# Denominators of linear attention: one row per head, spread over partitions by a DMA through DRAM

## The chip, the cores and the metric

The kernel runs on one core of one Trainium2 chip. The metric is the device time of one execution in microseconds (us). A run is an execution; where several were made, the median is quoted with the lowest and highest. A ratio is the mean time of one kernel's fast runs over the mean time of the other kernel's fast runs of the same rounds, so it is not quite the ratio of the medians that are quoted. A run counts as slow when it lies over 1.5% above the fastest run of the same kernel.

Engine names in the profile lines: PE is TensorE, PEld its weight loads, DVE VectorE, ACT ScalarE, POOL GpSimd, SP SyncE, which here only issues DMAs. A q after the name (SPq, ACTq) marks the issuing of DMAs.

## The reference

The block is adaLN, linear attention, adaLN, and a GEGLU feed-forward layer; S = 2048 tokens, D = 1024, 32 heads of 32, F = 3584. What matters here is the middle:

```python
pq, pk = (phi(q), phi(k))                       # per head: s x d, all positive
kv  = jnp.einsum('bhsd,bhse->bhde', pk, v)
z   = jnp.einsum('bhsd->bhd', pk)
num = jnp.einsum('bhqd,bhde->bhqe', pq, kv)
den = jnp.einsum('bhqd,bhd->bhq', pq, z)[..., None] + 1e-06
o   = num / den                                 # one denominator per token and head
x   = x + ga * (o.transpose(...).reshape(B, S, D) @ wo)
```

The kernel multiplies the transposed query features by 1/den, merges kv with wo into one 1024 x 1024 matrix ("the merge"), and runs one projection for all heads. There are 2048 x 32 denominators, but the product needs each of them on the 32 partitions of its head.

## The kernel before

Every operation is first recorded in a plan. A list scheduler with a cost model then orders the operations of VectorE, ScalarE, GpSimd and SyncE in 16 rounds and keeps the order that its model likes best; TensorE's order is as recorded. The program issues each engine's operations in exactly that order. Below it is called the recorded order.

```python
KEEP = 0.7                                     # damping of the due times from round to round
...
for i in range(2 * self.ROUNDS):
    forward(i >= self.ROUNDS)                  # keeps the best order of all rounds
...
return [self.ops[n] for _, n in best[1]]
```

The denominators, two groups of 128 query features by 512 tokens at a time:

```python
def den_pair(b, g, banks):                     # called 16 times
    psd = banks.pair()
    for i in range(2):                         # Dbd: block diagonal, z of each head repeated in 32 columns
        te.matmul(psd[:, i, :], lhsT=Dbd[:, g + i, :], rhs=pqT[b][:, g + i, :], start=True, stop=True)
    ac.activation(out=psd, in_=psd, func=AF.Ln, bias=eps6, scale=1.0)
    rden = rden_ring()
    ac.activation(out=rden, in_=psd, func=AF.Exp, scale=-1.0)      # 1/den = exp(-ln(den))
    o = pqT[b][:, g:g + 2, :]
    tt_op(o, o, rden, ALU.mult)
```

The matmul does the spreading: its result has each denominator on all 32 partitions of the head. Five of the 16 pairs stand in the merge, eleven in the projection:

```python
for i, stage in enumerate(stages):             # the merge, beside the last query products
    ...
    if 6 <= i < 6 + KD:
        if i in (6, 8, 10, 12, 13):
            den_pair(*den_todo.pop(0), psN)
        wp_step(i - 6)
...
for tt in range(NTT):                          # the projection, 16 tiles of 128 tokens
    if den_todo:
        den_pair(*den_todo.pop(0), psX)
    xt = wo_tile(tt, psX if tt == 0 else psC)  # loads x on SP, 16 matmuls, x + result on VectorE, store of x2
```

A projection tile takes its buffer from `x2_ring`, whose slots begin at 191 KB of each partition; the first tiles of the next stage (the row sums of the down weights, "b11") begin at 174 KB.

Of the kernel before, what the change touches and what calls it, by code (L numbers as in the profile page):

```python
# [11 lines left out]
BF16 = mybir.dt.bfloat16  # L12
F16 = mybir.dt.float16
AF = mybir.ActivationFunctionType
ALU = mybir.AluOpType
# [262 lines left out]
def kernel(  # L278
# [14 lines left out]
    P = 128  # L293
# [4 lines left out]
    S, D = x_in.shape  # L298
    F = B_w_gate.shape[1]
    KD = D // P  # L300
    JF = F // P
    TG = 512
    NG = S // TG
# [8 lines left out]
    DH = D // H  # L312
# [5 lines left out]
    KH = KD // 2  # L318
    NPR = JF // 2
    MW = 4 * NW  # L320
# [55 lines left out]
    def at(off, shape, dt):  # L376
        return Ring(off, shape, dt, 1)()
# [3 lines left out]
    maskbd = at(0.25, [P], F16)  # L381
# [20 lines left out]
    eps6 = at(1.78125, [1], FP32)  # L402
# [11 lines left out]
    srep = at(2.75, [KD, DH], BF16)  # L414
    garow = at(3.5, [D], F16)
    gbrow = at(3.5, [D], F16)
    Dbd = at(7.5, [KD, P], F16)
    mrow_ring = Ring(9.5, [NW], F16, 2)
    c8 = at(11.5, [P], BF16)

# [15 lines left out]
    pqT = [pq2[b // 2][:, b % 2] for b in range(4)]  # L436
# [7 lines left out]
    for o in (3.5, 194.25, 7.5, 120):  # L444
        wm1_ring.slots += Ring(o, [MW], BF16, 1).slots
    wm2_ring = Ring(27.75, [MW], BF16, 4)
    wm2_ring.slots += Ring(152, [MW], BF16, 3).slots + Ring(53, [MW], BF16, 1).slots
    qf_ring = Ring(176, [2, TG], FP32, 3)
    Wo_sb = at(11.75, [KD, D], BF16)
    ph_ring = Ring(198.25, [2, TG], F16, 4)  # L450
# [1 line left out]
    kvzacc = at(190, [KD, P + 1], FP32)  # L452
    KVbd = at(194.25, [KD, P], F16)
    KVbdT = at(196.25, [KD, P], F16)
    rden_ring = Ring(44, [2, TG], BF16, 3)
    bst_ring = Ring(206.25, [NBN, nc.vector.BN_STATS_DIM], FP32, 4)
    mv_ring = Ring(206.5, [nc.vector.BN_AGGR_DIM], FP32, 8)
    rstd_ring = Ring(206.625, [1], FP32, 8)
# [5 lines left out]
    def quarters(n, shape, dt):  # L464
# [25 lines left out]
    sub_a = [at(76 + 3.5 * j, [NPR // 2, HB], F16) for j in range(3)]  # L490
    sub_b = [at(189 + 3.5 * j, [NPR // 2, HB], F16) for j in range(4)]
    x2_ring = Ring(191, [D], BF16, 4)
    x2e_ring = Ring(144, [D], BF16, 3)
    xhe_ring = Ring(150, [D], F16, 3)
    junk = at(156, [D], BF16)
# [9 lines left out]
    psX, psW, psN = Banks(4, 7), Banks(4, 5), Banks(6, 7)  # L505
    psC, psB = Banks(0, 3), Banks(4, 7)

    scr_pool = ctx.enter_context(tc.tile_pool(name="scr", bufs=1, space=bass.MemoryType.DRAM))
    xh_scr = [[scr_pool.tile([TG, D], F16, name=f"xhs{g}_{h}", tag=f"xhs{g}_{h}") for h in range(2)]
              for g in range(NGR)]  # L510
    xa_scr = [scr_pool.tile([TG, D], F16, name=f"xas{b}", tag=f"xas{b}") for b in range(NG)]
    x2_scr = [scr_pool.tile([TG, D], BF16, name=f"x2s{b}", tag=f"x2s{b}") for b in range(NG)]
    t_scr = scr_pool.tile([P, 4, NPR, NW], F16, name="ts", tag="ts")
    u_scr = scr_pool.tile([P, NPR // 2, 3, 4, HB], F16, name="us", tag="us")
# [7 lines left out]
    te, ve, ac, gp, sy = (plan.on(e) for e in ("PE", "DVE", "ACT", "POOL", "SP"))  # L522
# [12 lines left out]
    def tt_op(out, a, b, op):  # L535
        ve.tensor_tensor(out=out, in0=a, in1=b, op=op)  # L536
# [410 lines left out]
    def kv_products(b, kb):  # L947
        glo, ghi = kb * GPB, min(KD, (kb + 1) * GPB)
        kvps = (psKV1 if b == 0 else psKV if b == 3 else QB)()[:, 0:GPB * (P + 1)].rearrange("p (g e) -> p g e", e=P + 1)
        for tl in range(TT):  # L950
            for g in range(glo, ghi):
                te.matmul(kvps[:, g - glo, :], lhsT=pks[b, tl // 2][:, tl % 2, g * P:(g + 1) * P],  # L952
                                 rhs=vta[:, tl][:, g, 0:P + 1], start=(tl == 0 and g == glo), stop=(tl == TT - 1),
                                 skip_group_check=True)
        src = kvps[:, 0:ghi - glo, :]
        if b == 0:
            ve.tensor_copy(out=kvzacc[:, glo:ghi, :], in_=src)
        else:
            tt_op(kvzacc[:, glo:ghi, :], src, kvzacc[:, glo:ghi, :], ALU.add)

    def den_pair(b, g, banks):
        psd = banks.pair()
        for i in range(2):
            te.matmul(psd[:, i, :], lhsT=Dbd[:, g + i, :], rhs=pqT[b][:, g + i, :], start=True, stop=True)
        ac.activation(out=psd, in_=psd, func=AF.Ln, bias=eps6, scale=1.0)  # L965
        rden = rden_ring()
        ac.activation(out=rden, in_=psd, func=AF.Exp, scale=-1.0)  # L967
        o = pqT[b][:, g:g + 2, :]
        tt_op(o, o, rden, ALU.mult)

    den_todo = [(b, g) for b in range(NG) for g in range(0, KD, 2)]

    def wp_step(g):
        psw = psW.pair()
        for h in range(2):
            te.matmul(psw[:, h, :], lhsT=KVbdT[:, g, :], rhs=Wo_sb[:, g, h * NW:(h + 1) * NW], start=True, stop=True)
        ve.scalar_tensor_tensor(out=Wp[:, g, :], in0=psw.rearrange("p h n -> p (h n)"), scalar=1.0 / GA_SCALE,
                                in1=garow, op0=ALU.mult, op1=ALU.mult)

    def kv_diagonal():  # L980
        for g in range(KD):
            ve.tensor_scalar_mul(out=Dbd[:, g, :], in0=maskbd, scalar1=kvzacc[:, g, P:P + 1])
        tt_op(KVbd, kvzacc[:, :, 0:P], maskbd[:, None, :].to_broadcast((P, KD, P)), ALU.mult)

    def kv_transposes():
        for half in range(2):
            psk = psX(F16)[:, 0:NW].rearrange("p (g e) -> p g e", e=P)
            for g in range(4):
                te.transpose(psk[:, g, :], KVbd[:, half * 4 + g, :], ident)
            ve.tensor_copy(out=KVbdT[:, half * 4:half * 4 + 4, :], in_=psk)  # L990
# [18 lines left out]
    def wd_moves(seen_of, n):  # L1009


        if not wd_todo:
            return
        plan.hold([op for op in plan.ops if op.eng == "PE"][-1])
        gp.tensor_copy(out=seen, in_=seen_of)
        plan.hold(plan.ops[-1])
        for dst, src, add in wd_todo[:n]:
            move(dst, src, add)
        del wd_todo[:n]
        plan.hold()  # L1020
# [98 lines left out]
    def ln2_xhat(tt, x2, mv, rstd):  # L1119
        g, h, tl = tt // (2 * TT), tt // TT % 2, tt % TT  # L1120
        xh = xh2_ring()
        ve.tensor_scalar(out=xh, in0=x2, scalar1=mv[:, 0:1], scalar2=rstd[:, 0:1],
                                op0=ALU.subtract, op1=ALU.mult)
        gp.dma_start(out=xh_scr[g][h][tl * P:(tl + 1) * P, :], in_=xh)
        if tl == TT - 1:
            h2_load(g, h)
# [44 lines left out]
    def wo_tile(tt, banks):  # L1171
        b, tl = tt // TT, tt % TT
        xt = x2_ring()
        sy.dma_start(out=xt, in_=x_in[tt * P:(tt + 1) * P, :])
        psw = banks.pair()
        for half in range(NHD):
            for g in range(KD):
                te.matmul(psw[:, half, :], lhsT=pqT[b][:, g, tl * P:(tl + 1) * P],  # L1178
                          rhs=Wp[:, g, half * NW:(half + 1) * NW], start=(g == 0), stop=(g == KD - 1))
        tt_op(xt, psw.rearrange("p h n -> p (h n)"), xt, ALU.add)  # L1180
        gp.dma_start(out=x2_scr[b][tl * P:(tl + 1) * P, :], in_=xt)
        return xt

    def merge_phase(stages):

        ms1 = ModSet(1, wm1_ring, psK)
        sy.dma_start(out=Wo_sb, in_=A_wo.rearrange("(kd p) n -> p kd n", p=P))
        for i, stage in enumerate(stages):
            if i < NKB:
                kv_products(NG - 1, i)  # L1190
            if i in (0, 2):
                for _ in range(KH):
                    ms1.step()
            if i == 3:
                ms2 = ModSet(2, wm2_ring, psN)
                ms1.columns()
            if i == 4:
                ms1.spread(0, garow, GA_SCALE)
                kv_diagonal()
            if i == 5:  # L1200
                kv_transposes()
            if i == 12:
                ms2.columns()
                ve.tensor_scalar_add(out=opcB, in0=modT[:, 4 * KD:5 * KD], scalar1=1.0)
            if 6 <= i < 6 + KD:
                if i in (6, 8, 10, 12, 13):
                    den_pair(*den_todo.pop(0), psN)
                wp_step(i - 6)
            if i == 11:
                for _ in range(KD):  # L1210
                    ms2.step()
            stage(())
            if 7 <= i < 11:
                wd_moves(Wp[:, i - 7, 0:1], 3)
        return lambda: ms2.spread(2, gbrow, 1.0)
# [3 lines left out]
    def wo_phase(gate_rows):  # L1219
        plan.transpose = (6000, 1000000)  # L1220
        fill = [None] * NTT
        fill[9] = h2_mods[0][0]
        fill[11] = h2_mods[0][1]
        fill[12] = h2_steps
        for tt in range(NTT):
            if den_todo:
                den_pair(*den_todo.pop(0), psX)
            xt = wo_tile(tt, psX if tt == 0 else psC)
            for h in range(2):
                if tt == AIM[h]:  # L1230
                    plan.aim(h2_loads[0, h])
            if tt == NTT - 2:
                gate_rows()
            if tt < 2 * TT:
                ln2_xhat(tt, xt, *ln2_stats(xt, act_rstd))
            for f in fill[tt] or []:
                f()
# [483 lines left out]
```

## Time and profile before

757.8 us, median of 3 runs (757.32 to 763.23).

| what | value | view |
|---|---|---|
| TensorE busy | 734.4 of 754.9 us (97%) | busy table |
| granted clock | 1.0 in every stretch | table of windows |
| TensorE idle from 165 to 254 us (merge end and projection) | 4.0 us | table of windows |
| 32 denominator matmuls | 0.216 us each when back to back, 6.9 us | timeline |
| 16 Ln and 16 Exp of 128x1024 | 1088 and 1024 ns, 33.8 us | source lines |

The head of the profile page, with the busy time and the forty slices in tenths:

```profile
span 754.9 us, 11379 instructions
...
PE 734.4 (97%) x4144; PEld 391.3 (52%) x4164; DVE 623.4 (83%) x1304; ACT 411.6 (55%) x697; POOL 95.8 (13%) x175
...
PE   5999999998999999999999999999999999999997
...
PEclk9999999999999999999999999999999999999999
```

The table of windows of the same run. Columns: the stretch in us, its length, busy us of each engine with instructions in brackets, granted clock, DMA share, GB/s:

```profile
165.00:195.00 30.00, 26.79 (x152) 12.01 (x153) 26.28 (x39) 25.59 (x28) 15.08 (x16) 1.00 0.78 130
195.00:254.00 59.00, 58.19 (x268) 26.41 (x270) 49.08 (x81) 36.27 (x53) 11.98 (x22) 1.00 0.86 253
254.00:754.00 500.00, 495.02 (x2854) 279.10 (x2856) 415.56 (x887) 250.96 (x485) 29.12 (x50) 1.00 0.58 180
```

254 us is where the first gate matmul of the feed-forward layer begins (253.7 by the timeline). I call what lies ahead of it "early" and what follows "late"; they sum to the span, up to rounding. The early part ends here after 253.7 us and the late one takes 501.3 us. In these two windows TensorE has 4.0 us of gaps in 89, so nearly all of its work counts in full; ScalarE has room.

The groups of waits by TensorE (engine and line, what it waited for: us in total, times, longest):

```profile
PE psum L964 <- ACT mem L967: 1.9, 2, 1.0
...
PE psum L1178 <- DVE mem L536: 0.7, 1, 0.7
```

L964 is the denominator matmul, L967 the Exp, L1178 the projection matmul, L536 a helper that records VectorE's products and sums. That is nearly all that TensorE waits in this part.

### The profile page before, as it was taken

To read this page: it belongs to the slowest core of one execution; us is meant where nothing else is said; L and a number is where in the kernel's file an instruction comes from. 1 tells how busy PE (TensorE), PEld (TensorE's weight loads), DVE (VectorE), ACT (ScalarE), POOL (GpSimd) and SP (SyncE) were. 2 spreads that over 40 slices of the span, in tenths; PEclk is the share of its full clock that TensorE was granted. 3 is DMA by queue.
4 is the path that set the end of the run, shared out by engine and by line. 5 is a ranking of instruction groups with operands and counts; after the bars stand their busy time and mean duration, and the time that the engine had idled before them with its cause. 6 is when DMAs were issued, how large, how long until landed. Compare 5 with 4: busy or idle time off the path is not lost.

```text
span 754.9 us, 11379 instructions
## 1 busy us (share of the span) xinstructions
PE 734.4 (97%) x4144; PEld 391.3 (52%) x4164; DVE 623.4 (83%) x1304; ACT 411.6 (55%) x697; POOL 95.8 (13%) x175
## 2 busy tenths in 40 slices
PE   5999999998999999999999999999999999999997
PEld 2454544453444444444545486645555555548664
DVE  7898986579897788988998689678888899998763
ACT  3675675668866578766755243016666667621000
POOL 2331332007121003101100001010000000000000
PEclk9999999999999999999999999999999999999999
DMA  9848166789389647687652999752322313399822
GB/s 314 305 120 252 43 151 155 277 309 167 86 231 315 232 154 246 220 272 281 207 185 60 292 276 313 254 181 84 112 78 90 112 56 112 103 274 294 280 95 80
DMA packets 140760, 144.78 MB, mean 192 GB/s; under 512 B 33441, under 2 KB 120865, under 8 KB 139937
## 3 DMA queue, kind: packets, MB, share of 16 engines
q1 hardware_dynamic: 124016, 106.31, 46.8%
q0 software_dynamic: 14336, 35.66, 14.9%
q10 hardware_dynamic: 2352, 2.10, 0.8%
q8 instruction: 32, 0.52, 0.3%
q14 instruction: 24, 0.19, 0.1%
HBM read 111.81 MB, written 32.24 MB: 191 GB/s over the span
## 4 chain that ended last, share of the span: by engine, by line
PE 80%; DVE 8%; ACT 6%; DMA 4%; issue 1%; SPq 1%; DVEq 0%; ACTq 0%
PE psum L1286 28%; PE psum L1489 13%; PE psum L1533 9%; PE psum L1297 7%; DVE mem L536 7%; PE psum L838 6%; PE psum L1178 6%; PE psum L908 4%; PE psum L937 4%; DMA mem<-in_A_wqkv_dram 2%; DMA mem<-in_B_w_up_dram 1%; DMA mem<-in_w_mod_dram 1%; PE psum L952 1%; ACT psum L965 1%; ACT mem L967 1%
## 5 line engine op out<-in xcount | busy, mean ns | idle before, releaser
L536 DVE TENSOR_TENSOR mem<-mem 128x512 f16<-128x512 f16 (+11 forms) x633 | 292.5, 506 | 12.1 <-ACT mem L967 2.5
L1286 PE MATMUL psum<-mem 128*128 128x512 f16 x1248 | 299.3, 379 | 1.3 <-ACT psum L1340 0.5
L536 DVE TENSOR_TENSOR mem<-psum,mem 128x512 f16<-128x512 f32 (+4 forms) x260 | 192.3, 748 | 67.5 <-ACT mem L783 22.6
L783 ACT ACTIVATE mem<-psum 128x256 f32<-128x256 f32 (+2 forms) x228 | 123.2, 555 | 121.1 <-PE psum L1533 46.4
L1286 PEld LDWEIGHTS <-mem 128*128 128x128 f16 (+1 forms) x1248 | 122.0, 98 | 113.4 <-issue 4.0
L1489 PE MATMUL psum<-mem 128*128 128x512 f16 (+2 forms) x458 | 99.0, 372 | 0.7 <-DVE mem L536 0.5
L1297 PE MATMUL psum<-mem 128*128 128x256 f16 x560 | 89.5, 272 | 0.3
L1297 PEld LDWEIGHTS <-mem 128*128 128x128 f16 (+1 forms) x560 | 54.7, 98 | 45.7 <-issue 3.9
L1489 PEld LDWEIGHTS <-mem 128*128 128x128 f16 x462 | 45.1, 98 | 49.9 <-issue 0.7
L1533 PE MATMUL psum<-mem 128*128 128x256 f16 (+1 forms) x588 | 66.2, 273 | 0.0
L1340 ACT ACTIVATE psum<-psum 128x512 f32<-128x512 f32 x56 | 33.0, 589 | 59.0 <-PE psum L1286 31.5
L1533 PEld LDWEIGHTS <-mem 128*128 128x128 f16 x588 | 57.5, 98 | 9.2
L838 PE MATMUL psum<-mem 128*128 128x512 f16 (+1 forms) x272 | 61.6, 379 | 0.4
L1178 PE MATMUL psum<-mem 128*128 128x512 f16 x256 | 57.4, 379 | 0.8 <-DVE mem L536 0.7
L908 PE MATMUL psum<-mem 128*128 128x512 f16 x224 | 51.1, 379 | 0.1
L536 DVE TENSOR_TENSOR psum<-psum,mem 128x256 f32<-128x256 f32 x80 | 34.2, 427 | 12.3 <-ACT mem L783 12.2
L1357 ACT ACTIVATE mem<-psum 128x512 f16<-128x512 f32 x56 | 33.2, 598 | 18.8 <-PE psum L1286 18.3
L838 PEld LDWEIGHTS <-mem 128*128 128x128 f16 x280 | 27.1, 98 | 31.2
L1178 PEld LDWEIGHTS <-mem 128*128 128x128 bf16 x256 | 25.0, 98 | 31.0 <-issue 0.9
L1367 ACT ACTIVATE mem<-mem 128x512 f16<-128x512 f16 x56 | 34.9, 633 | 2.0 <-DVE mem L536 1.8
L908 PEld LDWEIGHTS <-mem 128*128 128x128 f16 (+1 forms) x224 | 21.5, 98 | 26.8 <-issue 2.1
L614 DVE BATCH_NORM_STATS2 mem<-mem 128x6 f32<-128x512 bf16 x48 | 31.0, 678 | 1.6 <-DMA mem<-in_A_x_dram 1.6
(126 smaller groups left out, 558.5 us busy)
## 6 DMA issues: line engine op xcount, KB each, us to landing
mem<-in_B_w_gate_dram SPq DMA_DIRECT2D x14, 1024.0 KB, 6.1
mem<-in_B_w_up_dram SPq DMA_DIRECT2D x14, 1024.0 KB, 5.8
mem<-in_w_mod_dram SPq DMA_DIRECT2D x24, 512.0 KB, 7.0
mem<-us SPq DMA_DIRECT2D x24, 448.0 KB, 8.0
mem<-in_A_x_dram SPq DMA_DIRECT2D x32, 256.0 KB, 4.0
ts<-in_B_w_down_dram POOLq DMA_DIRECT2D x28, 256.0 KB, 6.7
us<-mem POOLq DMA_DIRECT2D x7, 768.0 KB, 7.2
mem<-in_B_w_down_dram SPq DMA_DIRECT2D x12, 448.0 KB, 6.8
```

The lines of the kernel that those rows point to most:

```text
L536: ve.tensor_tensor(out=out, in0=a, in1=b, op=op)
L783: ac.activation(out=t, in_=ps, func=AF.Copy)
L838: te.matmul(ps, lhsT=A[:, k, i * P:(i + 1) * P], rhs=B[:, k, :], start=(start and k == 0), stop=(k == KH - 1), skip_group_check=True)
L908: te.matmul(o, lhsT=W[:, k, (j0 + i) * P:(j0 + i + 1) * P], rhs=h_form(a, k), start=(start and k == 0), stop=(k == KH - 1), skip_group_che ...
L1178: te.matmul(psw[:, half, :], lhsT=pqT[b][:, g, tl * P:(tl + 1) * P], rhs=Wp[:, g, half * NW:(half + 1) * NW], start=(g == 0), stop=(g == K ...
L1286: te.matmul(ps, lhsT=a[:, k, e, :], rhs=b[:, k, :], start=(start and k == 0), stop=(k == KH - 1), skip_group_check=True)
L1297: te.matmul(ps, lhsT=self.x[a][:, k, :], rhs=self.y[y][:, k, :], start=(start and k == 0), stop=(k == KH // 2 - 1), skip_group_check=True)
L1340: ac.activation(out=z, in_=x, func=AF.Copy)
L1357: ac.activation(out=o, in_=ps, func=AF.Gelu_apprx_tanh)
L1367: ac.activation(out=o, in_=o, func=AF.Gelu_apprx_tanh)
L1489: te.matmul(psm[:, q, c], lhsT=A[:, i, q * P:(q + 1) * P], rhs=wt[:, i, c], start=(start and i == 0), stop=(i == NPR - 1), skip_group_chec ...
L1533: te.matmul(ps[:, q, :], lhsT=a[:, k, q * P:(q + 1) * P], rhs=y[:, k, :], start=(start and q == 0 and k == 0), stop=(k == NPR // 2 - 1), s ...
```

## The change

The intent: compute each denominator once, in one row per head, take Ln and Exp there, and let the DMA engines do the spreading. The new weights `zc` have 32 columns, so four sums fill the 128 partitions of one result, and 2 blocks of 512 tokens go through one pair of activations of 128x512. The inverses are stored to DRAM as [4 rows x 2048] for each block and half of the features. A load reads each row 32 times, 512 KB in all, into 128 partitions.

```diff
-    Dbd = at(7.5, [KD, P], F16)
+    zc = at(7.5, [KD, DH], F16)
+    rdc = at(8.5, [TG], BF16)
...
-    rden_ring = Ring(44, [2, TG], BF16, 3)
+    rden_ring = Ring(44, [KH, TG], BF16, 2)
+    rden_ring.slots += Ring(56, [KH, TG], BF16, 1).slots
...
     x2_ring = Ring(191, [D], BF16, 4)
+    x2_ring.slots += Ring(176, [D], BF16, 4).slots
...
+    def den_sums(pr, ps):                        # pr: the pair of token blocks
+        for gi in range(KH):
+            for b in range(2):
+                for half in range(2):
+                    o, g = DH * (2 * b + half), KH * half + gi
+                    te.matmul(ps[o:o + DH, :], lhsT=zc[:, g, :], rhs=pqT[2 * pr + b][:, g, :],
+                              start=(gi == 0), stop=(gi == KH - 1))
+        ac.activation(out=ps, in_=ps, func=AF.Ln, bias=eps6, scale=1.0)
+        ac.activation(out=rdc, in_=ps, func=AF.Exp, scale=-1.0)
+        for b in range(2):
+            for half in range(2):
+                o = DH * (2 * b + half)
+                sy.dma_start(out=den_scr[pr][b, half].rearrange("j (g t) -> (j g) t", g=KH),
+                             in_=rdc[o:o + KH * P // DH, :])
+
+    def den_mul(b, half):
         rden = rden_ring()
+        src = den_scr[b // 2][b % 2, half]
+        sy.dma_start(out=rden.rearrange("p g t -> p (g t)"),
+                     in_=src[:, None, :].to_broadcast((P // DH, DH, KH * TG)))
+        for i in range(0, KH, 2):
+            o = pqT[b][:, KH * half + i:KH * half + i + 2, :]
+            tt_op(o, o, rden[:, i:i + 2, :], ALU.mult)
...
-                if i in (6, 8, 10, 12, 13):
-                    den_pair(*den_todo.pop(0), psN)
+                if i == 6:
+                    den_sums(0, psN())
+                if i in (9, 11, 13):
+                    den_mul(*den_todo.pop(0))
...
-            if den_todo:
-                den_pair(*den_todo.pop(0), psX)
+            if tt == 1:
+                den_sums(1, psX())
+            if tt in (0, 2, 3, 5, 6):
+                den_mul(*den_todo.pop(0))
```

Cut: the DRAM scratch, the fill of `zc`, one moved slot of a weight ring, and the removed lines of `den_pair`, which is printed above.

More of the change, by code (lines that the diff above doesn't have):

```diff
@@ L446 @@
     wm2_ring = Ring(27.75, [MW], BF16, 4)
-    wm2_ring.slots += Ring(152, [MW], BF16, 3).slots + Ring(53, [MW], BF16, 1).slots
+    wm2_ring.slots += Ring(152, [MW], BF16, 3).slots + Ring(52, [MW], BF16, 1).slots
     qf_ring = Ring(176, [2, TG], FP32, 3)
@@ L511 @@
     xa_scr = [scr_pool.tile([TG, D], F16, name=f"xas{b}", tag=f"xas{b}") for b in range(NG)]
+    den_scr = [scr_pool.tile([2, 2, P // DH, KH * TG], BF16, name=f"den{pr}", tag=f"den{pr}") for pr in range(2)]
     x2_scr = [scr_pool.tile([TG, D], BF16, name=f"x2s{b}", tag=f"x2s{b}") for b in range(NG)]
@@ L959, in kv_products @@
             tt_op(kvzacc[:, glo:ghi, :], src, kvzacc[:, glo:ghi, :], ALU.add)
-    def den_pair(b, g, banks):
-        psd = banks.pair()
-        for i in range(2):
-            te.matmul(psd[:, i, :], lhsT=Dbd[:, g + i, :], rhs=pqT[b][:, g + i, :], start=True, stop=True)
-        ac.activation(out=psd, in_=psd, func=AF.Ln, bias=eps6, scale=1.0)
-        rden = rden_ring()
-        ac.activation(out=rden, in_=psd, func=AF.Exp, scale=-1.0)
-        o = pqT[b][:, g:g + 2, :]
-        tt_op(o, o, rden, ALU.mult)
-    den_todo = [(b, g) for b in range(NG) for g in range(0, KD, 2)]
+    def den_sums(pr, ps):
[13 more added lines that the diff above has]
+    def den_mul(b, half):
+        rden = rden_ring()
+        src = den_scr[b // 2][b % 2, half]
[4 more added lines that the diff above has]
+            tt_op(o, o, rden[:, i:i + 2, :], ALU.mult)
+    den_todo = [(b, half) for b in range(NG) for half in range(2)]
     def wp_step(g):
@@ L980, in kv_diagonal @@
     def kv_diagonal():
+        gp.memset(zc, 0.0)
         for g in range(KD):
-            ve.tensor_scalar_mul(out=Dbd[:, g, :], in0=maskbd, scalar1=kvzacc[:, g, P:P + 1])
+            ve.tensor_scalar_mul(out=zc[:, g, g % KH:KH * P // DH:KH], in0=maskbd[:, 0:P:DH], scalar1=kvzacc[:, g, P:P + 1])
         tt_op(KVbd, kvzacc[:, :, 0:P], maskbd[:, None, :].to_broadcast((P, KD, P)), ALU.mult)
```

## The prediction

> **What bounds the kernel now.** TensorE: in the page's busy table PE has 734.4 us of a 754.9 us span (97%). By the table of windows PE is idle 8.8 us in the first 20 us, 3.2 in the last 14, and 3.2 from 165 to 195 us, where the merge of the output weights runs beside the last query products. From 195 to 255 us, in the output projection, it is idle 0.8 us. The denominators live in these last two stretches; there VectorE is busy 26.3 of 30 us and 50 of 60, ScalarE 25.6 and 36.
>
> **What the change removes.**
> - ScalarE: 16 pairs of Ln (1088 ns) and Exp (1024 ns), 33.8 us. Four activations of 128x512 come instead, about 0.6 us each here: 2.4 us.
> - TensorE: 32 matmuls of 128x512 at 0.216 us (the timeline shows 0.43 us per pair between projection groups), 6.9 us. Instead, 32 matmuls with 32 output columns[...]. The modulation's 32 matmuls of 128*32 took 1.91 us. [...] TensorE saves 5.0 us: 1.2 in the merge, 3.8 in the projection.
> - VectorE: the 16 products of 128x1024 (0.68 us) stay; the diagonal's eight small products shrink, under 1 us.
>
> **What it adds.** Eight small stores and eight loads of 512 KB that spread the rows, all on SP's queue. Loads of 256 to 512 KB took 3.7 to 7.4 us from issue to landing in this window. From sum to first product: about 1.2 us of activations, 2 to 4 of store, 4 to 7 of load, 8 to 11 in all. The sums are issued at the sixth step, near 167 us; the first product stands on VectorE before the sixth of eight merge steps, near 177. That is tight, and the weight moves keep the DMA share at 0.7 to 1.2 then.
>
> **How much is critical.** In the projection PE has no gaps, so its 3.8 us count in full if VectorE follows: of a 3.88 us period it idles about 0.3, and at 3.45 it becomes the tighter engine for the first eight tiles. It can catch up in the last eight, which have no normalisation; but the second half's transposed rows come 1 to 2 us later against PE, with some 3 us of slack before the gate products. In the merge, 1.2 us of PE work and the waits on the Exp (1.9 + 0.2) go; VectorE's floor of about 27 us keeps part. The 0.7 us wait on VectorE near 239 us may go. The 31 us of ScalarE are mostly worth nothing.
>
> Sum: -5.0 (PE work), -2.5 (waits), +1.5 (new waits) = -6 us.
>
> **Prediction: 751.5 us, 747.5 to 756.** Faster by over 2%: 0.02; within 2%: 0.97; slower: 0.01.
>
> **What would show it.** Den matmuls under 2.5 us in all; ScalarE 31 us lower; PE 5 us lower; no PE wait on the Exp; projection tiles 3.45 us apart; VectorE waiting under 3 us on the spread rows; gate products from about 247 instead of 253.7 us, the rest unchanged within 1 us.
>
> **What would make it wrong.** The first spread load landing late, so that VectorE and the merge stop for several us; stores and loads holding up SP's queue before input tiles or transposes; the new recorded order costing time in the gate and up stage.

The 5.0 us of TensorE are 6.9 us less the 1.91 us that before's trace shows for 32 matmuls of 128*32. The 2 to 4 us of store were a guess of mine; no trace is named for them.

## The result, and the profile after

787.88 us median (787.28 to 790.06, 4 runs) against 758.66 before: ratio 1.0379, 95% interval 1.033 to 1.0428. The change made the kernel 3.8% slower. The result is correct.

The head of the page after:

```profile
span 788.3 us, 11367 instructions
...
PE 742.3 (94%) x4148; PEld 391.1 (50%) x4164; DVE 623.2 (79%) x1304; ACT 381.9 (48%) x669; POOL 96.5 (12%) x176
...
PE   5999999996977799999999999999999999999997
...
PEclk9999999998988899999999999999999999999999
```

ScalarE lost 29.7 us, as foreseen. But TensorE's busy time rose by 7.9 us although it has less to do, and slices 10 to 14 have gaps or a lower clock. The table of windows after, cut at the same events (the first gate matmul begins at 280.7 us):

```profile
165.00:195.00 30.00, 22.65 (x131) 9.07 (x131) 18.60 (x27) 12.55 (x15) 14.95 (x16) 0.89 0.81 154
195.00:281.00 86.00, 68.85 (x286) 28.70 (x286) 50.67 (x82) 19.34 (x37) 12.30 (x22) 0.88 0.79 207
281.00:788.00 507.00, 495.71 (x2854) 278.93 (x2856) 420.76 (x898) 251.01 (x486) 30.51 (x50) 1.00 0.57 179
```

The early part is 27.0 us longer. TensorE is busy 22.65 + 68.85 = 91.5 us there instead of 26.79 + 58.19 = 85.0, so 6.5 us of the 27 are busy time and 20.5 idle time. The late part is 6.3 us longer at the same busy time.

The waits of TensorE and VectorE after:

```profile
PE psum L1198 <- DVE mem L540: 15.9, 4, 7.2
...
PE psum L568 <- DVE mem L563: 4.8, 1, 4.8
PE psum L995 <- DVE mem L996: 3.2, 3, 2.5
```

```profile
DVE mem L540 <- DMA mem<-den: 31.8, 6, 7.4
```

L1198 is now the projection, L995 the merge, L568 a small matmul of the modulation, L540 the helper. The wait of 31.8 us by VectorE is for the spread rows. It didn't exist before, and I had allowed it 3 us. The timeline of VectorE shows the first two of the six:

```profile
179.68 0.41 DVE L782 TENSOR_SCALAR mem<-mem 128x1024 f16<-128x1024 f16 x1
185.21 0.69 DVE L540 TENSOR_TENSOR mem<-mem 128x1024 bf16<-128x1024 bf16 x1 [5.12 <-DMA mem<-den]
...
193.47 0.69 DVE L540 TENSOR_TENSOR mem<-mem 128x1024 bf16<-128x1024 bf16 x1 [4.63 <-DMA mem<-den]
```

And the queue that issues, SP, at the same time (L978 the stores, L984 the spread loads, L1194 the x tiles):

```profile
170.89 1.74 SPq L978 DMA_DIRECT2D den<-mem  x4
172.74 3.37 SPq L984 DMA_DIRECT2D mem<-den  x2
...
206.40 1.72 SPq L978 DMA_DIRECT2D den<-mem  x4
...
218.88 1.16 SPq L984 DMA_DIRECT2D mem<-den  x2
```

The first load was issued at 172.74 and its product began at 185.21, 12.5 us later; the load was what the product waited for. For the second pair of blocks the stores alone landed 12.1 to 12.5 us after they were issued, and the loads could be issued only then; why the stores were so slow wasn't taken apart.

TensorE's timeline shows the second effect. After a stall, 16 projection matmuls took 6.56 us; before, 16 of them took 3.62 us (from the start of the first to the end of the last). The table of windows gives 0.50 as the granted clock around the end of the first stall (184.1 to 188.9 us):

```profile
231.71 6.56 PE L1198 MATMUL psum<-mem 128*128 128x512 f16 x16 [5.84 <-DVE mem L540]
240.97 12.21 PE L1198 MATMUL psum<-mem 128*128 128x512 f16 x48 [2.69 <-DVE mem L540]
260.40 9.33 PE L1198 MATMUL psum<-mem 128*128 128x512 f16 x32 [7.23 <-DVE mem L540]
```

```profile
186.60:193.30 6.70, 4.17 (x13) 1.60 (x15) 2.23 (x4) 0.00 (x0) 0.73 (x1) 0.50 1.03 213
```

In the clock records of the trace there are five stretches at 0.5, of 6.83, 3.41, 6.83, 3.41 and 6.83 us, 27.3 us in all. Each begins in the last 2.4 us of one of TensorE's five stalls of over 2 us, or at most 0.8 us after it. They account for the busy time: 6.5 us more, although 4.8 us of matmul work are gone (below), makes 11.3 us; and TensorE is busy for 21.7 us of these 27.3, of which half, 10.8 us, is what half clock adds.

### The profile page after: what moved, and what is told of

Same layout as the page of the kernel before. It is cut to its first block, busy times and chain, and to the rows that moved or that the text cites. A ratio compares the mean times of both kernels' runs of the same rounds, so it can differ in the third digit from the quotient of the medians.

```text
span 788.3 us, 11367 instructions
## 1 busy us (share of the span) xinstructions
PE 742.3 (94%) x4148; PEld 391.1 (50%) x4164; DVE 623.2 (79%) x1304; ACT 381.9 (48%) x669; POOL 96.5 (12%) x176
## 4 chain that ended last, share of the span: by engine, by line
PE 49%; DMA 8%; DVE 6%; ACT 4%; issue 1%; SPq 0%; DVEq 0%; ACTq 0%
PE psum L1310 24%; PE psum L1513 12%; PE psum L1557 6%; PE psum L1321 6%; DVE mem L540 5%; DMA mem<-xhs 4%; DMA mem<-x2s 2%; DMA mem<-in_B_w_up_dram 1%; PE psum L1198 1%; ACT mem L787 1%; ACT mem L1178 1%; DVE psum L540 1%; ACT psum L1364 1%; ACT mem L1163 1%; ACT mem L1159 0%
## 5 line engine op out<-in xcount | busy, mean ns | idle before, releaser
L540 DVE TENSOR_TENSOR mem<-mem 128x1024 f16<-128x1024 bf16 (+11 forms) x633 | 294.6, 507 | 46.9 <-DMA mem<-den 31.8
L1310 PE MATMUL psum<-mem 128*128 128x512 f16 x1248 | 299.6, 379 | 3.2 <-ACT mem L787 1.6
L540 DVE TENSOR_TENSOR mem<-psum,mem 128x512 f16<-128x512 f32 (+4 forms) x260 | 192.3, 748 | 62.1 <-ACT mem L787 24.4
L787 ACT ACTIVATE mem<-psum 128x256 f32<-128x256 f32 (+2 forms) x228 | 123.3, 554 | 119.2 <-PE psum L1557 46.8
L1198 PE MATMUL psum<-mem 128*128 128x512 f16 x256 | 63.7, 413 | 15.9 <-DVE mem L540 15.9
L1557 PEld LDWEIGHTS <-mem 128*128 128x128 f16 x588 | 57.5, 98 | 11.3 <-issue 2.1
L912 PE MATMUL psum<-mem 128*128 128x512 f16 x224 | 54.2, 395 | 0.2
L1198 PEld LDWEIGHTS <-mem 128*128 128x128 bf16 x256 | 26.7, 105 | 52.8 <-issue 27.8
L540 DVE TENSOR_TENSOR psum<-psum,mem 128x256 f32<-128x256 f32 x80 | 34.2, 427 | 14.7 <-ACT mem L787 14.4
## 6 DMA issues: line engine op xcount, KB each, us to landing
mem<-in_A_x_dram SPq DMA_DIRECT2D x32, 256.0 KB, 9.4
ts<-in_B_w_down_dram POOLq DMA_DIRECT2D x28, 256.0 KB, 7.0
```

Source lines behind the costliest of these rows:

```text
L540: ve.tensor_tensor(out=out, in0=a, in1=b, op=op)
L787: ac.activation(out=t, in_=ps, func=AF.Copy)
L912: te.matmul(o, lhsT=W[:, k, (j0 + i) * P:(j0 + i + 1) * P], rhs=h_form(a, k), start=(start and k == 0), stop=(k == KH - 1), skip_group_che ...
L1198: te.matmul(psw[:, half, :], lhsT=pqT[b][:, g, tl * P:(tl + 1) * P], rhs=Wp[:, g, half * NW:(half + 1) * NW], start=(g == 0), stop=(g == K ...
L1310: te.matmul(ps, lhsT=a[:, k, e, :], rhs=b[:, k, :], start=(start and k == 0), stop=(k == KH - 1), skip_group_check=True)
L1557: te.matmul(ps[:, q, :], lhsT=a[:, k, q * P:(q + 1) * P], rhs=y[:, k, :], start=(start and q == 0 and k == 0), stop=(k == NPR // 2 - 1), s ...
```

## The experiments

The first theory, A in the expectations: the load's shape makes it slow. Its source has 4 rows, and between 180 and 192 us its packets (4096 bytes each, about 172 ns) are never more than 4 at a time. Theory A supposes that more source rows bring more packets in flight and a faster load; the change's trace alone doesn't show that. (The trace doesn't name a packet's engine, so how many DMA engines carry the load isn't shown.) The rivals: the repeated reading of the same rows of DRAM; the queue of SP; and the recorded order, which the scheduler made anew for the whole kernel.

A table of all runs comes first; "early" and "late" are read from the profiled run of each, and the medians of before in its five batches of rounds are 758.94 (e1 to e4), 757.02 (e5 to e8), 758.13 (e9 to e11), 757.97 (e12 to e14) and 757.77 (e15, e16). The batches ran on four different chips, so times of different batches are best compared by their ratios to before.

| run | median us (lowest to highest) | ratio to before [95%] | early | late |
|---|---|---|---|---|
| before | 758.66 (757.32 to 763.23) | 1 | 253.7 | 501.3 |
| the change | 787.88 (787.28 to 790.06) | 1.0379 [1.033, 1.0428] | 280.7 | 507.6 |
| e1 no spread | 768.60 (767.76 to 775.16) | 1.0139 [1.0088, 1.019] | 249.7 | 516.8 |
| e2 8 rows | 777.33 (776.09 to 780.43) | 1.0241 [1.0204, 1.0278] | 266.9 | 507.4 |
| e3 16 rows | 767.26 (763.22 to 772.81) | 1.0118 [1.0051, 1.0184] | 252.6 | 511.0 |
| e4 4 loads of one row | 771.20 (769.68 to 773.53) | 1.0157 [1.0121, 1.0194] | 264.4 | 507.4 |
| e5 no spread, old late order | 761.63 (759.27 to 762.34) | 1.0054 [1.0029, 1.0078] | 257.5 | 501.7 |
| e6 16 rows, old late order | 766.09 (764.37 to 767.77) | 1.0118 [1.0092, 1.0143] | 259.7 | 503.0 |
| e7 the change, old late order | 792.29 (789.7 to 796.53) | 1.0469 [1.0431, 1.0507] | 287.5 | 507.3 |
| e8 before, other order | 774.45 (763.83 to 782.93) | 1.0144 [1.0077, 1.0211] | 252.8 | 517.7 |
| e9 no spread, whole old order | 758.85 (757.75 to 762.12) | 1.0021 [0.9983, 1.0058] | 256.0 | 500.6 |
| e10 16 rows, whole old order | 771.48 (769.38 to 776.86) | 1.0187 [1.0141, 1.0234] | 267.9 | 500.6 |
| e11 the change, whole old order | 796.35 (794.02 to 796.84) | 1.0498 [1.0471, 1.0526] | 290.3 | 504.8 |
| e12 no spread, four slots | 754.91 (753.74 to 758.67) | 0.9955 [0.9899, 1.001] | 249.2 | 502.6 |
| e13 16 rows, ACT's queue | 773.51 (771.41 to 774.89) | 1.0189 [1.0135, 1.0243] | 266.2 | 503.4 |
| e14 16 rows, SP and ACT | 762.79 (762.32 to 764.86) | 1.0059 [0.9998, 1.012] | 259.7 | 500.8 |
| e15 16 rows, SP and POOL | 757.68 (755.32 to 763.08) | 1.0002 [0.9959, 1.0046] | 260.1 | 501.2 |
| e16 e15, gate products moved | 755.87 (754.21 to 761.06) | 0.9961 [0.9939, 0.9983] | 255.1 | 504.2 |

### The load itself: e1, e2, e3, e4

e1 takes the stores and loads away. The product multiplies the tile by itself instead, with the same instruction, so its result is wrong.

```diff
-                sy.dma_start(out=den_scr[pr][b, half].rearrange("j (g t) -> (j g) t", g=KH),
-                             in_=rdc[o:o + KH * P // DH, :])
...
-        sy.dma_start(out=rden.rearrange("p g t -> p (g t)"),
-                     in_=src[:, None, :].to_broadcast((P // DH, DH, KH * TG)))
...
-            tt_op(o, o, rden[:, i:i + 2, :], ALU.mult)
+            tt_op(o, o, o, ALU.mult)
```

> No stores, no spread loads; each product multiplies a tile with itself (wrong result on purpose, same size and count of VectorE work). All theories in which the spread's DMA is the cause expect the compute part alone to be a gain: 749 to 753 us, PE busy about 729 us, no stall over 1 us between 165 and 240 us, clock 1.0. A rival in which the compact sums themselves, the 32-column matmuls or the new recorded order cost the time expects over 775 us.

e2 and e3 keep the 512 KB load and give its source 8 and 16 rows, by storing each head's row two or four times; the sum makes two copies by two equal columns of `zc`, and e3 stores twice.

```diff
-    den_scr = [scr_pool.tile([2, 2, P // DH, KH * TG], ...
+    den_scr = [scr_pool.tile([2, 2, 4 * P // DH, KH * TG], ...      # e2: 2 * P // DH
...
-                sy.dma_start(out=den_scr[pr][b, half].rearrange("j (g t) -> (j g) t", g=KH),
-                             in_=rdc[o:o + KH * P // DH, :])
+                for s in range(2):
+                    sy.dma_start(out=den_scr[pr][b, half].rearrange("(j s r) (g t) -> s j (r g) t", s=2, r=2, g=KH)[s],
+                                 in_=rdc[o:o + DH, :])
...
-                     in_=src[:, None, :].to_broadcast((P // DH, DH, KH * TG)))
+                     in_=src[:, None, :].to_broadcast((4 * P // DH, DH // 4, KH * TG)))
```

> Each compact row is stored twice, so the spread load reads 8 rows 16 times instead of 4 rows 32 times; same bytes, same place in the DMA queue. Theory A [...]: at most 8 packets of 4096 bytes in flight instead of 4, a load's packets take about 4 us instead of 8, VectorE's wait on the spread rows falls from 31.8 to under 10 us, time 755 to 768. Rival B (the round trip through DRAM has a fixed latency, lengthened by the weight moves, and the products stand too early): waits and time stay within 3 us of 788. Rival C (many reads of one DRAM row are slow): something between.

> As e2, but 16 rows read 8 times each, with two stores per group (8 more small stores on SP). Theory A: up to 16 packets in flight, a load in about 2 to 3 us, wait on the spread rows under 4 us, time 750 to 756. Rival B: stays near 788. Rival C: faster than e2, so it does not tell A from C.

e4 keeps the four rows, each read 32 times, and splits the load into four loads of one row to 32 partitions. It is the control for the rival that reading the same row again and again is slow. That theory A expects a fast spread here was my assumption; no trace had shown it.

```diff
-        sy.dma_start(out=rden.rearrange("p g t -> p (g t)"),
-                     in_=src[:, None, :].to_broadcast((P // DH, DH, KH * TG)))
+        for j in range(P // DH):
+            sy.dma_start(out=rden.rearrange("p g t -> p (g t)")[DH * j:DH * j + DH, :],
+                         in_=src[j:j + 1, :].to_broadcast((DH, KH * TG)))
```

> The source stays 4 rows, each read 32 times, but every load is issued as four, one per row, to 32 partitions each; 24 more issues of about 0.5 us on SP. Theory A: [...] the spread is fast, 750 to 760 us. Rival C (many reads of one DRAM row): still slow, over 775, as the reads of a row stay 32. Rival B: over 785.

What was measured. VectorE's wait for spread rows, which was 31.8 us in the change, from the waits of e2, e3 and e4:

```profile
DVE mem L540 <- DMA mem<-den: 6.7, 4, 3.6
```

```profile
DVE mem L540 <- DMA mem<-den: 3.0, 2, 2.4
```

```profile
DVE mem L540 <- DMA mem<-den: 4.2, 2, 3.4
```

With 4, 8 and 16 rows the wait is 31.8, 6.7 and 3.0 us. In the loads of the first pair, the packets in flight at a time go up to 4, 8 and 14 (5 in one load of the change), and the 128 packets of a load take 8.5 to 8.7 us, 4.4 to 5.2 us and 3.8 to 4.2 us. So 16 rows gain little over 8, less than the 2 to 3 us that I had expected. A fixed latency of the way through DRAM (rival B of the expectations) would have left the wait as it was. e4 reads the same four rows as often as the change and waits 4.2 us. So it is the shape of the one load from four rows that makes it late, and the repeated reading isn't. The early part falls from 280.7 us to 266.9, 252.6 and 264.4 us. In e4 it stays long with short waits for the rows: TensorE waits 12.9 us for VectorE in three stalls. Ahead of the second VectorE waits 3.4 us for spread rows, and ahead of the third 4.0 us for ScalarE, which had waited 9.1 us for transposed rows. The first I did not take apart; the 24 more issues on SP may be part of it.

All four totals missed their ranges: e2 to e4 by 9 to 11 us above them, and e1, at 768.60, lies between its two readings. The late part is longer than before's in all four, 507 to 517 us against 501.3; in e3 that is the whole loss, as its early part is 1.1 us shorter than before's.

e1 says what remains when the spread costs nothing: its gate products begin 4.0 us earlier than before's (249.7 against 253.7), yet it is 1.4% slower, because its late part takes 15.5 us more. The change has no operation in that part. TensorE's timeline of e1 shows the largest loss (L1550 is a matmul of the down projection):

```profile
451.74 2.24 PE L1550 MATMUL psum<-mem 128*128 128x256 f16 x19
462.17 3.15 PE L1550 MATMUL psum<-mem 128*128 128x256 f16 x14 [8.19 <-ACT mem L787]
```

And ScalarE's, around it:

```profile
460.12 1.52 ACT L1171 ACTIVATE mem<-mem 128x512 f16<-128x512 f16 x2 [11.75 <-DMA mem<-xhs]
461.54 0.57 ACT L787 ACTIVATE mem<-psum 128x512 f32<-128x512 f32 x1
```

ScalarE's order has two activations of the second half's normalised rows ahead of a copy (L787) for which TensorE waits. The rows are transposed by a DMA and landed at 460.1 us, so ScalarE and then TensorE stood still; a stretch of 10.24 us at half clock began during that stall (14 of these matmuls took 3.15 us after it; 19 had taken 2.24 us before). That is a matter of the recorded order.

### The recorded order: e5, e6, e7, e8

e5 (wrong, as e1), e6 and e7 are e1, e3 and the change, with every operation from the first gate product on put into the order that the scheduler gave before. The kernel carries the start times which the scheduler worked out for before, and sorts by them. The two causes that the expectations of e6 and e7 weigh are the four-row load and the new order; e7's first reading put them at about 18 and 10 us.

```diff
-        return [self.ops[n] for _, n in best[1]]
+        return self.grafted(best[1])     # late operations: sorted by before's start times, dependences kept
...
+    plan.mark = len(plan.ops)            # the late part begins here
     gate_up(0)
```

> As e1 (no stores, no spread loads, wrong result on purpose), but every operation of the gate, up and down stages is issued in the order that the kernel before records for them; only the first part keeps its own order. If e1 loses its 4 us head start (gate products at 249.7 instead of 253.7 us) because the planner, re-run on a changed program, records a worse order for the rest (the two normalisation activations put ahead of a copy cost an 8.2 us wait and half clock after it), this run is 750 to 755 us and shows no wait over 2 us after 300 us. If the loss comes from the earlier start itself or from elsewhere (memory traffic, weights that arrive late against TensorE), it stays over 762 us.

> e3 (16-row source, correct result) with the late stages in the order of the kernel before. If both causes are right and add up [...]: 750 to 757 us, TensorE at full clock throughout. If the order is not a cause: 763 to 768 as e3.

> The change as it stands (4-row source) with the late stages in the order of the kernel before. [...] 772 to 782 us; waits of VectorE on the spread rows stay near 32 us. If the spread is nearly all of the loss: 785 to 790.

e8 is the control from the other side: the kernel before, operation for operation, with one constant of the scheduler changed so that it finds another order.

```diff
-    KEEP = 0.7
+    KEEP = 0.68
```

> A control: the kernel before, with one damping constant of its planner changed (0.70 to 0.68) and nothing else, so that the same operations are recorded in another order. If the order that the planner happens to record is worth about 10 us (the kernel before carries a selected one): 762 to 772 us, with new waits in the gate, up and down stages. If recorded orders are all alike: within 2 us of the kernel before.

The late part came back to 501.7 us in e5 and 503.0 in e6, from 516.8 and 511.0. In e8 it went from 501.3 to 517.7 us with not one operation changed. Two of e8's four runs (776.58 and 782.93) count as slow, and the ratio of 1.0144 rests on the other two (763.83 and 772.32). So the 501 us of before belong to one good order, and any edit that makes the scheduler start afresh can lose over 10 us. In e7 the late part stays at 507.3 us. Its trace has a TensorE stall of 2.5 us at 416 us, behind VectorE's wait of 2.7 us for a load of up weights, and 3.41 us at half clock after it: about 4 of the 5.6 us over e5. Why that load came late is open.

But the early parts of e5, e6 and e7 grew by 7.8, 7.1 and 6.8 us, which took back half of e5's late gain and most of e6's; e7 had gained only 0.3 us. So e5's total lies between its two readings, e6's in the range that I had named for "the order is not a cause", and e7's above both of its ranges; it is the late parts that show the order as a cause, not the totals. I put the growth down to late operations that now interleave differently with the end of the projection. The traces of the three have a wait there that e1, e3 and the change don't have, of VectorE for a store of x2 rows (6.3, 5.7 and 7.0 us; here e5's). e12 below removes it.

```profile
DVE mem L573 <- DMA x2s<-mem: 6.3, 1, 6.3
```

This is why I gave the early part the old order too.

### The whole recorded order: e9, e10, e11

Each operation that isn't part of the denominators has before's start time as its key, the four products of a group have the times of before's products, and the sums, stores and loads follow TensorE. The second group of sums moves from the second projection tile to the third, since e1 showed a TensorE wait of 2.1 us at these sums. e10's first reading was that the 16-row spread does no harm once its products stand late enough.

```diff
-        return [self.ops[n] for _, n in best[1]]
+        return self.spliced()            # all operations sorted by before's start times, dependences kept
...
-            if tt == 1:
+            if tt == 2:
                 den_sums(1, psX())
```

> As e1 (no stores, no spread loads, wrong result on purpose), but the whole program is issued in the order that the kernel before records, with only the new denominator operations spliced in: sums of the second pair one tile later, first products moved 1 to 9 us later. If my first estimate was right for the arithmetic and only the order and the transfers spoil it: 750 to 754 us, gate products from 247 to 250 us and 501 to 503 us from there to the end. If the faster projection cannot be used because the transposed rows come no earlier: gate products at 252 or later, time 754 to 758.

> The correct kernel with 16-row sources and the whole order of the kernel before, denominators spliced in as in e9. [...] within 3 us of e9, 751 to 757 us, VectorE waiting under 2 us on the spread rows. If the 4 MB of spread loads still delay the transposed rows: 3 to 10 us over e9, with TensorE waiting for VectorE behind the activations of the transposed rows.

> As e10 with the change's own 4-row source; nothing else differs but the stores and the rows. Theory A [...]: 15 to 28 us slower than e10, most of it before the gate products, with VectorE waiting on the spread rows or behind the transposed rows. If the order was the real cause of the loss: within 5 us of e10.

e11 against e10 is the cleanest measure of the four-row load: same order, same rounds, 796.35 against 771.48 us, 24.9 us. The other two such pairs agree: 26.2 us (e7 and e6) and 20.6 us (the change and e3, with orders of their own). VectorE's waits for spread rows in e11 and e10:

```profile
DVE mem L584 <- DMA mem<-den: 14.6, 4, 5.7
```

```profile
DVE mem L584 <- DMA mem<-den: 3.7, 1, 3.7
```

But e10 missed: it is 12.6 us over e9, and its early part is 15.3 us longer than e3's with the same transfers. VectorE waits 6.8 us for x tiles and 6.4 us for a store of x2 rows in e10 and for neither in e3, so before's order brings back the late part and costs the early one. e9, which has no spread at all (and so a wrong result), only equals before (1.0021). So the load and the order together are not the whole story. The waits of e9 name one more thing: VectorE waits for a store of x2 rows, and TensorE, ahead of the last projection tile, for VectorE.

```profile
DVE mem L584 <- DMA x2s<-mem: 6.8, 1, 6.8
PE psum L1243 <- DVE mem L584: 5.2, 1, 5.2
```

The change had given `x2_ring` four more slots at 176 to 184 KB. There the next stage's first tile ("b11", from 174 KB) is written while the projection's last rows are still being stored. Before's ring doesn't overlap with it. The change itself has no such wait. It stands only in runs that carry before's order in part or whole (e5 to e7 and e9 to e11), so it is no part of the change's 3.8%.

### Four slots again, and other queues: e12, e13, e14

e12 is e9 without the four extra slots; its result is wrong too.

```diff
     x2_ring = Ring(191, [D], BF16, 4)
-    x2_ring.slots += Ring(176, [D], BF16, 4).slots
```

> No stores and no spread loads (wrong result on purpose), the whole recorded order of before, and the x2 ring back at its four slots of before. Theory that the change's four extra ring slots, which share space with the first gate tiles, caused the 5.16 us TensorE wait and the half clock after it in e9: that wait is gone, the first gate product begins at 247 to 250 us, the total is 748 to 752 us. Rival that the remaining stall has another cause (the order itself, or the stores of x2 being late for other reasons): about 758 us as in e9, with a wait over 4 us still at the first gate product.

e13 and e14 are correct: e10 with four slots, with start times of their own for the loads, and with the stores and loads issued elsewhere. e13 issues all from ScalarE; e14 issues the first pair from SP, ahead of the x loads, and the second from ScalarE.

```diff
-                    sy.dma_start(out=den_scr[pr][b, half]...
+                    (ac if pr else sy).dma_start(out=den_scr[pr][b, half]...      # e13: ac
...
-        sy.dma_start(out=rden.rearrange("p g t -> p (g t)"), ...
+        (ac if b > 1 else sy).dma_start(out=rden.rearrange("p g t -> p (g t)"), ...   # e13: ac
```

> Correct result: 16-row sources, whole order of before, four ring slots, all den stores and loads issued from ScalarE's queue. Theory that in e10 the den transfers held up the x loads behind them in SyncE's queue: VectorE no longer waits 6.8 us for x tiles, waits for spread rows stay under 6 us in all, and the total is 752 to 762 us. Rival that the time from sums to product is itself the limit wherever the transfers are issued: waits for spread rows of over 8 us, a TensorE wait of over 4 us with half clock after it, and 766 us or more.

> Correct result: as e13, but the first pair's den transfers are issued from SyncE ahead of the x loads that block there, the second pair's from ScalarE. Theory (queueing): 750 to 758 us, waits for spread rows under 5 us in all, at most one TensorE wait over 2 us before the gate products. Rival (time from sums to product): 766 us or more, as in e10.

In e12 the stall and the wait for the x2 stores are gone, the clock is 1.0 from the start-up to the last matmuls, the gate products begin at 249.2 us, and the median is 754.91 us. That is 3.9 us under e9, but in other rounds. The ratios are 0.9955 and 1.0021, and their intervals overlap, so the removed stall rests on the traces. It is 2.9 us above the 748 to 752 that I had expected. Its waits of TensorE from 150 to 290 us show what took the place of the Exp (L1242 is its projection, L1037 its merge):

```profile
PE psum L1242 <- DVE mem L583: 2.4, 1, 2.4
PE psum L1037 <- DVE mem L1038: 1.9, 2, 1.3
```

This run is what the arithmetic is worth when the spread is free: about 3 us (0.9955, with an interval that just includes 1).

e13 missed: at 773.51 us it is no better than e10. ScalarE's timeline says why (L1023 the stores):

```profile
169.37 5.70 ACTq L1023 DMA_DIRECT2D den<-mem  x8
175.12 1.02 ACT L925 ACTIVATE mem<-psum 128x1024 f16<-128x1024 f32 x1 [5.78 <-DMA den<-mem]
```

ScalarE computes nothing for 5.70 us because it issues eight small stores, 0.71 us each. TensorE waits 5.5 us for that activation. The wait for x tiles is 6.3 us, so the queue theory got no support from e13 either. e14 has one such block instead of two, and is at 762.79 us; its VectorE waits only 1.0 us for spread rows and 0.6 us for x tiles, and its TensorE stalls twice:

```profile
PE psum L1254 <- DVE mem L583: 6.5, 2, 3.7
```

```profile
201.47 5.71 ACTq L1024 DMA_DIRECT2D den<-mem  x8
207.22 0.29 ACT L674 ACTIVATE mem<-mem 128x1 f32<-128x1 f32 x1 [5.79 <-DMA den<-mem]
```

Note that the profile writes this block down as a wait for a DMA, though it is issuing time. From e10 to e14 three things changed at once (slots, queue and order of the loads), so their 8.7 us are not divided among them; e14's total, too, lies between its two readings (750 to 758, and 766 or more).

### Issuing without ScalarE: e15, e16

e15 is e14 with the second pair's stores issued from GpSimd. e16 is e15 with four products of VectorE, which scale the first gate weights and wait for a weight load, recorded after the last two projection tiles and not ahead of them.

```diff
-                    (ac if pr else sy).dma_start(out=den_scr[pr][b, half]...
+                    (gp if pr else sy).dma_start(out=den_scr[pr][b, half]...      # e15, e16
...
+    # e16 alone: start times of the four products, 234.3 to 236.2 -> 239.1 to 240.9 in the scheduler's count
```

> Correct result: e14 with the second pair's eight stores issued from GpSimd in place of ScalarE. Theory that issuing them held up ScalarE by 5.7 us and so VectorE (5.34 us for the layer norm scale) and TensorE (3.68 us, then 6.83 us of half clock): this TensorE wait falls under 1 us, and the total is 754 to 758 us (762.8 less 3.7 and 3.4). Rival that the second pair's spread comes late wherever its stores are issued: VectorE waits over 3 us for spread rows and the total stays at 760 us or more.

> Correct result: e15, and VectorE's four products of the first gate weights, which wait for a weight load, recorded after the last two projection tiles in place of ahead of them. Theory that they held up the projection's last tiles: the TensorE wait of 2 to 3 us near 235 to 245 is gone with its half clock, 1.5 to 5 us under e15, so 750 to 755 us. Rival that TensorE then waits for the gate weights themselves at the first gate product: a wait of over 2 us there, and no gain over e15.

e15 is at 757.68 us, equal to before and 5.1 us under e14, which ran in other rounds; the intervals of the two ratios overlap. The traces of the two show what changed: the activation L674, which had waited 5.79 us in e14, follows the Exp at once, and TensorE runs 80 projection matmuls there without a stall.

```profile
203.15 0.28 ACT L674 ACTIVATE mem<-mem 128x1 f32<-128x1 f32 x1
```

```profile
201.84 17.44 PE L1254 MATMUL psum<-mem 128*128 128x512 f16 x80
```

e16 is at 755.87 us, ratio 0.9961 with an interval of 0.9939 to 0.9983: a correct version that beats before by 0.4% (and the change by some 4%). By the bar of 2% it counts as the same as before. The difference of 1.8 us between e16 and e15 is within what I had expected, but their ranges overlap, and I don't call it shown. Nor did the stall go that the move was to remove: in e16's profile TensorE still waits 2.86 us ahead of its last projection tile, now behind VectorE's wait for normalised rows.

```profile
246.19 1.06 DVE L1253 TENSOR_SCALAR mem<-mem 128x512 f16<-128x512 f16 x3 [3.46 <-DMA mem<-xhs]
```

```profile
249.97 5.30 PE L1271 MATMUL psum<-mem 128*128 128x512 f16 x16 [2.86 <-DVE mem L600]
```

The profiled runs of e16 and e15 are the slowest of each (761.06 and 763.08 us), so their early times are not those of a typical run. In e16's profile two half-clock stretches are left, 3.41 us each, behind stalls of 2.86 and 1.99 us.

## Why the prediction was wrong

The prediction said 751.5 us (747.5 to 756), and 0.01 for slower by over 2%. It came out at 787.88 us.

What held:

- "Den matmuls under 2.5 us in all": a group of 16 sums took 1.05 us where nothing held it up (the change's second group had a wait of 0.28 us in it), 2.1 us for both instead of 6.9, so 4.8 us saved against 5.0 predicted. That is 66 ns a sum, where a denominator matmul of before took 216 ns. "ScalarE 31 us lower": 29.7 us.
- "Projection tiles 3.45 us apart": so they are where nothing waits. No TensorE wait on the Exp is left.
- "Gate products from about 247": 249.2 us in e12 and 249.7 us in e1, where the spread is free.

What failed, as the prediction put it:

- "4 to 7 [us] of load, 8 to 11 in all". This is the step that broke it. I had costed the load by its size, from loads of 256 to 512 KB in this window that took 3.7 to 7.4 us. The first one took 12.5 us from issue to product, and the shape of its source is the cause: the same 512 KB from 8 and 16 rows cut VectorE's wait from 31.8 to 6.7 and 3.0 us (e2, e3), and 24.9 us lie between e11 and e10. I hadn't asked what the shape does, nor measured a load of this shape. The "2 to 4 of store" in the same chain failed too, in the second pair: 12.1 to 12.5 us.
- "+1.5 (new waits)". VectorE's new waits were 31.8 us, and TensorE's stalls that they left in this part 15.9 + 4.8 + 3.2 = 23.9 us. On top came a term that the sum didn't have: with each of the five stalls of over 2 us the clock fell to 0.5 for 3.41 or 6.83 us, 11.3 us of longer matmuls in all.
- "-2.5 (waits)". The 2.1 us of waits on the Exp went, but in e12 waits of 2.4 and 1.9 us came in their place. This term is about zero, and with it the arithmetic is worth 3 to 4.5 us, not 6.
- "The rest unchanged within 1 us". The late part took 6.3 us more, and 15.5 us more in e1. e8 shows that the order alone can do this, at 16.4 us. I had named the order as a risk and given it no size.
- SP's queue: also named, and not sized. With 16 rows the correct version still lost 8 to 13 us (e3, e6, e10). In e3 that is the late part, so the order; in e6 and e10 it is the early part, until the slots, the place and queue of the loads and the issuing time on ScalarE were mended together (e14, e15). What SP's queue alone cost isn't shown.

So the prediction named the three risks and gave all three together one chance in a hundred. A chain of sums, activations, store, load and product, in a place where TensorE has 4 us of gaps in 89, has a large downside and a gain of at most 6 us. That calls for a wide and lopsided range.

What stays open: what the three mended items between e10 and e14 are worth each; the first of e4's three stalls; why the second pair's stores took 12 us; the late load of up weights in e7 (507.3 us against 501.7 in e5); and the 6.3 us of the change's own late part, for which the order is the likely cause but no run isolates it.

## What to carry to other kernels

Before a DMA takes over a broadcast, measure its load in the shape that it will have: here VectorE waited 31.8 us for loads of 512 KB from 4 rows, 6.7 from 8 and 3.0 from 16, and storing each row several times (to get 16) made the kernel 20.6 to 26.2 us faster than the four-row load. Count in the time for issuing many small stores on an engine that computes (5.70 us for eight on ScalarE in e13), and a stall of TensorE at more than its length where half clock can follow: the change's five stalls of over 2 us, 23.1 us in all, brought 27.3 us at half clock (the next section has stalls without it). In a kernel with a scheduled order, a control that changes only the order belongs to every experiment, or a gain of a few us can't be told from a new draw.

## What else the traces showed

- Half-clock stretches are 3.41, 6.83 or 10.24 us long here. They came with stalls of TensorE of 2.50, 2.69, 4.82, 5.84 and 7.23 us (the change, clock records) and of 1.97 us (e1: the 8 matmuls at 327.92 us took 3.01 us, the 8 at 322.20 us 1.89 us). They didn't come with stalls of 1.87 and 1.93 us (the change: granted clock 1.00 from 354 to 366 and from 484 to 495 us), 2.41 us (e12: 1.00 from 195 to 249 us) and 2.73 us (e3: the 16 matmuls after it took 3.61 us, as at full clock). So the length of a stall alone doesn't separate them; what does isn't shown.
- In the first pair's loads 4 packets (once 5) were in flight with 4 source rows, 8 with 8, and 12 to 14 with 16; among the second pair's, where other transfers run, 7 and 10 with 4 and 8 rows. VectorE's wait for these 512 KB loads was 31.8, 6.7 and 3.0 us with 4, 8 and 16 rows. What makes a load from few rows slow isn't shown.
- For a row of small stores the time for issuing added up: eight of 32 KB took 5.70 us of ScalarE to issue (e13), and with them on GpSimd the total was 5.1 us lower (e14 to e15, in other rounds). In e16 such stores landed 2.1 to 3.6 us after issue.
- The profile can write issuing time down as a wait for a DMA: in e14 the 5.79 us "<-DMA den<-mem" of ScalarE are 5.71 us of issuing.
